# First block of a convolution and SiLU kernel: 64 by 64 convolution tiles, taps spread by transpositions, silu ahead of the weight splits

## The chip, the cores and the metric

The kernel runs on one core of a Trainium2 chip. The metric is the device time of one execution in microseconds; lower is better. The inputs are random with a fixed seed.

## The reference

`x` has 8 sequences of 4096 tokens with 192 channels. A causal depthwise convolution with 7 taps comes first, where 24 channels share one head's taps, normalized by a softmax; then an up projection to 2048, SiLU, and a down projection back to 192. The two projection weights come as float64.

```
w = softmax(weight, axis=-1)                     # (8 heads, 7 taps)
x_pad = concatenate([zeros(B, 6, D), x], axis=1)
x_unf = x_pad[:, idx, :].reshape(B, S, 7, 8, 24)  # 7 shifted views
conv = einsum('hk,bskhg->bshg', w, x_unf)         # (8, 4096, 192)
h = conv.reshape(32768, 192) @ w_in               # (32768, 2048)
out = (h * sigmoid(h)) @ w_out                    # (32768, 192)
```

## The kernel before

**Blocks.** The 32768 tokens are worked in blocks of 1024 (`TT`), each in two halves of 512 (`TB`). Channels lie on the partitions: the first 128 channels of a block in `nats[0]`, and the last 64, the tail, in `nats[1]`, with the two halves of the tokens on partitions 0 to 63 and 64 to 127. Tokens come from memory in 32 by 32 squares that VectorE transposes (`turn_in`). From block 1 on, a planned order written out as a string (`PLAN`) sets the order of every instruction; the up matmuls there use weights that were split into three parts (`w_a`, `w_b`), and fewer products by a fast matrix scheme. Block 0 is another path, ahead of the plan, and the change touches that path alone, but for the order of the channels in `load` and in the up weights.

**Block 0 now.** Its steps in program order, which each engine's queue keeps for its own share:

- The tap logits and the first 128 channels of 1024 tokens are loaded, the latter by four DMAs (two on SyncE's queue, two on ScalarE's), so that each of four partition groups `q` holds 256 tokens. Then SyncE loads the raw up weights for `j` = 0 to 3 (`load_in`; part 0 is the first 128 rows, part 1 the last 64) with the four tail loads between.
- Three heat matmuls on zeros (`heat`) run on TensorE. The softmax of the taps runs on VectorE and ScalarE; three small matmuls with selection matrices spread the taps over the channels (into `banks[6]` and `banks[7]`).
- `turn_q` transposes the four squares of channels into `x_q`; `diagonals` makes diagonal matrices of the taps; `conv_on_pe` runs the convolution of the first 128 channels on TensorE as 7 x 4 x 4 matmuls of 32 by 32, 256 columns each; `conv_taken` copies the four banks to `x_first[0]` on ScalarE. Every such float32 matmul appears as two records in the profile.
- The tail's convolution (`conv(0, 1, i)`) has its first tap on ScalarE and the other six on VectorE.
- The raw weights are float64 words that are rounded to float32 by integer operations: a `Unit` each for part 0 and part 1 of each `j` (units 0 to 7, even for part 0) and one for each quarter of the down weights (units 8 to 11). `work(u)` yields twice: first `begin(u + 1)` (exponent on VectorE and GpSimd, sign on ScalarE), mantissa and sticky of `u`, then `rounded` (three VectorE operations, the last writes `wd`), `top` on ScalarE and, for odd units, `spread`, two DMAs from one half of the partitions to the other. `split` makes the three parts for later blocks (two VectorE operations, one of ScalarE).
- `up_both(0)` runs the up matmuls of `j` = 0: eight banks with the first 128 channels, then the same banks with the tail, then eight silu on ScalarE. `up_first(j, c)` does four banks at a time for `j` = 1 to 3. All eight banks of PSUM are in use by `up_both`.
- The list `rest` (weight units 2 to 9 and their splits) and the list `ups` are merged by `woven`, by costs, into one program order. As written, `top` of units 2 and 3 and the first split come ahead of the silu of `up_both`.
- `down_plain` does the down matmuls of block 0, after which the plan begins with block 1.

```
ups = pieces(up_both(0), 72, 18, 18)
ups += [f for j in range(1, NJ) for c in (0, 2) for f in pieces(up_first(j, c), 36 - 9 * c, 18 + 9 * c)]
woven(rest, ups)
```

Nearly every instruction is issued through a helper, so the profile shows line 142 for all engines but TensorE, line 494 (`mm`) for matmuls and line 400 for `heat`; the tiles tell them apart (`nat`: x in rows, `xt`: x transposed, `wd`: rounded weights, `ps`: PSUM, `g`: silu results and scratch).

Of the kernel before, what the change touches and what calls it, by code (L numbers as in the profile page):

```python
# [8 lines left out]
F32 = mybir.dt.float32  # L9
# [9 lines left out]
def kernel(  # L19
# [166 lines left out]
    nats = [const.tile([P, n, SQ], F32, name=f"nat{i}") for i, n in enumerate((TT // SQ, TB // SQ))]  # L186
    TQ = TT // 4
    GQ = P // SQ
    x_q = const.tile([P, GQ, pad + TQ], F32, name="xt0")
    xts = [flat(x_q)[:, 0 : pad + TT], const.tile([P, pad + TB], F32, name="xt1")]  # L190
# [9 lines left out]
    def load(b, i, queue, cols=slice(0, None)):  # L200
        i, small = i % 4, i // 4
        dst = nats[small][SQ * i : SQ * i + SQ]
        if small:
            c = P + SQ * (i % 2)
            queue.dma_start(out=dst, in_=x_v[2 * b + i // 2][:, :, c : c + SQ])
        else:
            queue.dma_start(out=dst[:, cols], in_=x_w[b][:, cols, SQ * i : SQ * i + SQ])

    NG = D // SQ
    HG = H * NG  # L210
    nat_q = flat(nats[0]).rearrange("p (k g c) -> p k g c", g=GQ, c=SQ)
    wexp = const.tile([HG, K], F32, name="wexp")
    sync.dma_start(out=wexp, in_=weight.unsqueeze(0).to_broadcast([NG, H, K]))
    for q in range(4):
        src = x.flatten_outer_dims()[q * TQ : q * TQ + TQ, 0:P].rearrange("(k t) c -> t k c", t=SQ)
        to = flat(nats[0])[SQ * q : SQ * q + SQ].rearrange("p (k c) -> p k c", c=P)
        (act if q % 2 else sync).dma_start(out=to, in_=src)
# [7 lines left out]

    sel = const.tile([HG, NG + 2, SQ], F32, name="sel")
    sel_q = const.tile([HG, 4, SQ], F32, name="selq")
    mask = const.tile([HG, GQ], F32, name="mask")
    one_hot = const.tile([P, SQ], F32, name="hot")
    pool.memset(sel, 1.0)  # L230
    pool.memset(mask, 1.0)
    vec.memset(one_hot, 0.0)
    for sign in (1, -1):
        pool.affine_select(
            out=sel[:, 0:NG],
            in_=sel[:, 0:NG],
            compare_op=ALU.is_ge,
            fill=0.0,
            base=0 if sign > 0 else grp - 1,
            pattern=[[sign * (SQ + H * grp), NG], [sign, SQ]],  # L240
            channel_multiplier=-sign * grp,
        )
    for sign in (1, -1):
        pool.affine_select(
            out=mask,
            in_=mask,
            compare_op=ALU.is_ge,
            fill=0.0,
            base=0 if sign > 0 else H - 1,
            pattern=[[-sign * H, GQ]],  # L250
            channel_multiplier=sign,
        )
    for q in range(4):
        pool.affine_select(
            out=one_hot,
            in_=one_hot,
            compare_op=ALU.not_equal,
            fill=1.0,
            base=-SQ * q,
            pattern=[[-1, SQ]],  # L260
            channel_multiplier=1,
        )
    pool.memset(x_q[0:SQ, :, 0:pad], 0.0)
# [4 lines left out]
    in_a = moe_w_in.bitcast(I32)[0:P].rearrange("p (a m c) -> p a m c", a=2, c=2 * P)  # L268
# [145 lines left out]
    taps_all = banks[6][:, 0 : GQ * K].rearrange("p (g i) -> p i g", i=K)  # L414
    w_norm = const.tile([HG, K], F32, name="wnorm")
    spread_logits = const.tile([HG, GQ, K], F32, name="wspread")
    wred = const.tile([HG, 3], F32, name="wred")
    top, total, part_ = (wred[:, i : i + 1] for i in range(3))
    heat(3)
    vec.tensor_reduce(top, wexp, axis=AX.X, op=ALU.max, negate=True)  # L420
    act.activation(wexp, wexp, AF.Exp, bias=top, accum_out=total)
    act.activation(warm, warm, AF.Silu)
    vec.tensor_reduce(sel_q[:, 0, :], sel[:, 0:GQ, :].rearrange("r g c -> r c g"), axis=AX.X, op=ALU.add)
    vec.tensor_copy(sel_q[:, 1:4, :], sel_q[:, 0, :].unsqueeze(1).to_broadcast([HG, 3, SQ]))
    vec.tensor_copy(sel[:, NG : NG + 2, :], sel[:, NG - 2 : NG, :])
    vec.tensor_scalar(total, total, scalar1=1e-9, scalar2=None, op0=ALU.add)
    vec.reciprocal(part_, total)
    vec.scalar_tensor_tensor(
        out=spread_logits,
        in0=wexp.unsqueeze(1).to_broadcast([HG, GQ, K]),  # L430
        scalar=part_,
        in1=mask.unsqueeze(2).to_broadcast([HG, GQ, K]),
        op0=ALU.mult,
        op1=ALU.mult,
    )
    vec.tensor_scalar(w_norm, wexp, scalar1=part_, scalar2=None, op0=ALU.mult)
    pin(nc.tensor.matmul(banks[6][:, 0 : GQ * K], flat(sel_q), flat(spread_logits), start=True, stop=True))
    for k in (1, 0):
        of = flat(sel[:, 4 * k : 4 * k + 4, :])
        pin(nc.tensor.matmul(banks[7][:, K * k : K * k + K], of, w_norm, start=True, stop=True))  # L440
    heat(1)

    def turn_q(g):
        for g_ in (g, g + 1):
            vec.transpose(x_q[:, g_, pad:], nat_q[:, :, g_, :])
# [4 lines left out]
    turn_q(0)  # L450
    turn_q(2)
# [423 lines left out]
```

## Time and profile before

| | |
|---|---|
| median of 3 runs | 2237.4 us (2235.35 to 2238.51) |
| the profiled execution | 2236.91 us |
| its span, first to last instruction | 2235.2 us |
| mean granted TensorE clock | 0.999 |
| TensorE busy | 2218.2 us (99%) |
| VectorE busy | 1826.7 us (82%) |
| ScalarE busy | 1292.0 us (58%) |
| GpSimd busy | 50.6 us (2%) |

In the profile PE is TensorE's matmuls and PEld its weight loads, DVE is VectorE, ACT ScalarE, POOL GpSimd and SP SyncE, which here only issues DMAs; a q after the name stands for the engine's queue. Times count from the first instruction. A row of the timeline gives start, length, engine, line, operation, tiles (out<-in), shape, count, and in brackets the idle time before and what ended it; "issue" means nothing that the profile shows. Ends of matmuls are modelled, so rows overlap a little.

### The profile page before, as it was taken

How to read it: one execution, taken by the hardware profiler on the slowest of the kernel's cores; microseconds unless marked ns; L12 is line 12 of the kernel's file. 1: busy time of each engine (PE TensorE's matmuls, PEld its weight loads, DVE VectorE, ACT ScalarE, POOL GpSimd, SP SyncE). 2: the span in 40 equal slices, each digit the busy share in tenths (PEclk: the TensorE clock that was granted, in tenths of full speed). 3: DMA queues.
4: the chain of work that ended last, by engine and by line, in shares of the span. 5: the costliest groups of instructions: out<-in, count | busy, mean ns of one | idle time of the engine just before them, and what ended most of it. 6: DMA issues, size and time to landing. Idle time of an engine off the chain costs nothing.

```text
span 2235.2 us, 47341 instructions
## 1 busy us (share of the span) xinstructions
PE 2218.2 (99%) x19406; PEld 1632.6 (73%) x19406; DVE 1826.7 (82%) x3029; ACT 1292.0 (58%) x2648; POOL 50.6 (2%) x73
## 2 busy tenths in 40 slices
PE   8999999999999999999999999999999999999998
PEld 4377777777777777777777777777777777777776
DVE  8787888877888778888778887788887788877877
ACT  5267555666555675556665556755466654567543
POOL 4300000000000000000000000000000000000000
PEclk9999999999999999999999999999999999999999
DMA  4311011110011110111101111101111011111001
GB/s 130 69 25 29 6 26 29 30 30 15 16 30 29 30 29 6 26 29 30 30 14 17 30 29 30 29 3 28 30 29 30 13 18 29 29 29 30 3 14 29
DMA packets 405007, 61.77 MB, mean 28 GB/s; under 512 B 398134, under 2 KB 403254, under 8 KB 404790
## 3 DMA queue, kind: packets, MB, share of 16 engines
q1 hardware_dynamic: 401046, 58.10, 14.9%
q8 instruction: 151, 2.47, 0.5%
q10 hardware_dynamic: 3744, 0.66, 0.2%
q14 instruction: 66, 0.54, 0.1%
HBM read 31.46 MB, written 25.17 MB: 25 GB/s over the span
## 4 chain that ended last, share of the span: by engine, by line
PE 98%; DVE 1%; ACT 0%; issue 0%; ACTq 0%
PE ps L494 98%; DVE g L142 0%; DVE nat L142 0%; DVE wd L142 0%; DVE fin L142 0%; ACT nat L142 0%; DVE dot L142 0%; DVE w_a L142 0%; ACT ps L142 0%; ACT fin L142 0%; ACT w_a L142 0%; ACT g L142 0%; ACT w_b L142 0%; ACT xt L142 0%; ACTq L142 0%
## 5 line engine op out<-in xcount | busy, mean ns | idle before, releaser
L494 PE MATMUL ps<-g,wd 128*64 128x256 f32 (+1 forms) x10112 | 1125.6, 384 | 0.0
L494 PEld LDWEIGHTS ps<-g,wd 128*64 128x64 f32 x10112 | 720.4, 137 | 395.6 <-issue 34.1
L142 DVE TENSOR_TENSOR g<-g 128x1024 f32<-128x1024 f32 x806 | 951.5, 1219 | 9.2 <-PE ps L494 5.6
L494 PE MATMUL ps<-xs,w_a 64*128 64x512 f32 x5952 | 848.7, 390 | 1.3 <-DVE dot L142 0.9
L142 ACT ACTIVATE ps<-ps 128x512 f32<-128x512 f32 (+1 forms) x1085 | 569.9, 585 | 298.4 <-PE ps L494 252.0
L494 PEld LDWEIGHTS ps<-xs,w_a 64*128 64x128 f32 x5952 | 592.6, 184 | 108.6 <-DVE dot L142 14.8
L142 ACT ACTIVATE g<-ps 128x512 f32<-128x512 f32 x1024 | 562.2, 619 | 57.2 <-PE ps L494 50.1
L494 PE MATMUL ps<-xs,w_b 64*128 64x512 f32 x2976 | 501.0, 391 | 0.0
L142 DVE COPY dot<-ps 128x1 f32<-128x1 f32 x992 | 156.1, 157 | 353.9 <-PE ps L494 344.7
L142 DVE SCALAR_TENSOR_TENSOR nat<-xt,taps,nat 128x512 f32<-128x512 f32 (+1 forms) x378 | 373.5, 1002 | 5.1 <-ACT nat L142 4.6
L494 PEld LDWEIGHTS ps<-xs,w_b 64*128 64x128 f32 x2976 | 302.3, 184 | 53.0 <-issue 11.5
L142 ACT COPY fin<-ps 128x256 f32<-128x256 f32 (+1 forms) x127 | 47.9, 377 | 410.7 <-PE ps L494 410.7
L142 DVE TENSOR_TENSOR fin<-fin,ps 128x256 f32<-128x256 f32 x248 | 96.2, 407 | 17.0 <-PE ps L494 17.0
L142 DVE STREAM_TRANSPOSE fin<-fin 128x256 f32<-128x256 f32 (+1 forms) x189 | 83.4, 442 | 7.5 <-ACT fin L142 6.0
L142 ACT ACTIVATE nat<-xt,taps 128x512 f32<-128x512 f32 (+1 forms) x63 | 58.7, 935 | 16.0 <-DVE xt L142 14.6
L142 DVE STREAM_TRANSPOSE xt<-nat 128x1024 f32<-128x1024 f32 (+2 forms) x67 | 62.0, 930 | 2.6 <-DMA nat<-in_x_dram 2.5
L142 DVE TENSOR_TENSOR xs<-nat,xs 128x1024 fp32r<-128x1024 f32 (+1 forms) x62 | 59.0, 952 | 0.0
L142 DVE SCALAR_TENSOR_TENSOR xs<-xs 128x1024 fp32r<-128x1024 f32 (+1 forms) x62 | 59.0, 951 | 0.1
L142 ACT ACTIVATE xs<-nat 128x1024 fp32r<-128x1024 f32 (+1 forms) x62 | 52.5, 847 | 10.9 <-DVE nat L142 10.9
L142 ACT ACTIVATE fin<-ps 128x256 f32<-128x256 f32 x93 | 35.9, 386 | 39.0 <-PE ps L494 37.6
L494 PE MATMUL ps<-nat,wd 128*128 128x512 f32 (+1 forms) x128 | 44.7, 613 | 6.1 <-ACT g L142 4.7
L142 ACT COPY xt<-xt 64x6 f32<-64x6 f32 (+2 forms) x63 | 12.4, 197 | 64.5 <-DVE xt L142 63.7
(63 smaller groups left out, 257.3 us busy)
## 6 DMA issues: line engine op xcount, KB each, us to landing
out_dram<-fin SPq DMA_DIRECT2D x242, 96.0 KB, 2.5
nat<-in_x_dram SPq DMA_DIRECT2D x126, 128.0 KB, 2.9
nat<-in_x_dram SPq DMA_DIRECT2D x128, 64.0 KB, 2.2
g<-in_moe_w_out_dram SPq DMA_DIRECT2D x4, 384.0 KB, 4.3
w_b<-w_b SPq DMA_DIRECT2D x8, 192.0 KB, 3.0
fin<-in_moe_w_out_dram SPq DMA_DIRECT2D x4, 384.0 KB, 3.8
g<-in_moe_w_in_dram SPq DMA_DIRECT2D x2, 512.0 KB, 6.0
fin<-in_moe_w_in_dram SPq DMA_DIRECT2D x2, 512.0 KB, 8.2
```

Source lines behind the costliest of these rows:

```text
L142: return lambda *args, **kw: pin(getattr(self.engine, name)(*args, **kw))
L494: return pin(nc.tensor.matmul(to, lhs, rhs, start=start, stop=True, skip_group_check=True))
```

## The change

Five things change, all in or ahead of block 0:

1. The first 128 channels of block 0 are loaded as 64-channel rows into another layout (`nat_m`, `x_m`): partition group `i` holds token half `h` and channel half `s`. Each group comes in two DMAs, early (8 or 9 squares of 32 tokens) and late (8). The late ones of groups 0 and 2 are issued by SyncE behind the first `load_in`, those of groups 1 and 3 by ScalarE behind the Exp.
2. With this layout the channels of the first 128 stand in blocks of 32 in the order 0, 2, 1, 3 (`ORDER`); `load` and `load_in` part 0 follow it, and the latter becomes four DMAs of 32 partitions each instead of one of 128.
3. The taps are spread without matmuls: VectorE copies the logits to four partition groups, normalizes, transposes 32 by 32, copies along the channels of a head, and transposes again; GpSimd copies the results to `taps`. There are seven heat matmuls instead of three plus one.
4. The convolution on TensorE is 64 by 64: per token half (early, late) 7 x 2 x 2 matmuls of 256 columns, with seven separate diagonal instructions; the late transpositions stand between the two halves. `conv_taken` is called for banks 0 and 2, then, after the first tap of the tail and unit 0's rounding, for banks 1 and 3.
5. `up_both` with its silu comes whole ahead of the rest, with only the first piece of unit 2's work inside; the splits come later (`SPLIT_AFTER`), most of them behind unit 7.

```diff
+    ORDER = (0, 2, 1, 3)
+    TL = SQ + TB
+    nat_m = const.tile([P, TL // SQ, 2, SQ], F32, name="nat0")
+    x_m = const.tile([P, 2, TL], F32, name="xt0")
...
+    w32 = const.tile([P, SQ], F32, name="w32")
+    logits = w32[:, 0:K]
+    vec.memset(w32, 0.0)
+    sync.dma_start(out=w32[0:H, 0:K], in_=weight)
+
+    def load_first(i, late, queue):
+        h, s = divmod(i, 2)
+        lo, hi = (8, 16) if late else (-h, 8)
+        src = x.flatten_outer_dims()[TB * h + SQ * lo : TB * h + SQ * hi, R * s : R * s + R]
+        to = nat_m[SQ * i : SQ * i + SQ, 1 + lo : 1 + hi].rearrange("t k g c -> t k (g c)")
+        queue.dma_start(out=to, in_=src.rearrange("(k t) c -> t k c", t=SQ))
+
+    for i in range(4):
+        load_first(i, False, act if i % 2 else sync)
...
-            queue.dma_start(out=to, in_=in_a[:, :, 2 * j : 2 * j + 2, :])
+            for i in range(4):
+                of = in_a[ORDER[i], :, :, 2 * j : 2 * j + 2, :]
+                queue.dma_start(out=to[SQ * i : SQ * i + SQ], in_=of)
...
     load_in(0, 0, sync)
+    for i in (0, 2):
+        load_first(i, True, sync)
     for i in range(4, 8):
         load(0, i, sync)
     load_in(0, 1, sync)
...
-    heat(3)
+    heat(7)
+    for q in range(1, 4):
+        vec.tensor_copy(w32[SQ * q : SQ * q + H, 0:K], w32[0:H, 0:K])
+    vec.tensor_reduce(top, logits, axis=AX.X, op=ALU.max, negate=True)
+    act.activation(logits, logits, AF.Exp, bias=top, accum_out=total)
+    for i in (1, 3):
+        load_first(i, True, act)
     act.activation(warm, warm, AF.Silu)
...
+    vec.tensor_scalar(logits, logits, scalar1=part_, scalar2=None, op0=ALU.mult)
+    vec.transpose(turned, w32)
+    vec.tensor_copy(
+        by_channel.rearrange("p (h c) -> p h c", c=grp), turned[:, 0:H].unsqueeze(2).to_broadcast([P, H, grp])
     )
+    vec.transpose(flat(taps_all), by_channel)
+
+    def turn_first(late):
+        at_ = slice(9, 17) if late else slice(0, 9)
+        for g in range(2):
+            vec.transpose(x_m[:, g, SQ * at_.start : SQ * at_.stop], nat_m[:, at_, g, :])
...
-    def conv_on_pe():
+    def conv_on_pe(late):
         for i in reversed(range(K)):
-            for g in range(GQ):
-                for q in range(4):
-                    at_ = slice(SQ * q, SQ * q + SQ)
-                    to = banks[q][SQ * g : SQ * g + SQ, 0:TQ]
-                    mm(to, diags[at_, i, g, :], x_q[at_, g, i : i + TQ], i == K - 1)
-        homes.extend([homes.pop(0) for q in range(4)])
+            at_ = SQ - pad + i + HT * late
+            for g in range(2):
+                for h in range(2):
+                    to = rows(banks[2 * h + late], g)[:, 0:HT]
+                    w = rows(diags[:, i, g].rearrange("p s c -> p (s c)"), h)
+                    mm(to, w, rows(x_m[:, g, at_ : at_ + HT], h), i == K - 1)
...
-    conv_on_pe()
+    conv_on_pe(0)
+    turn_first(True)
+    conv_on_pe(1)
     begin(0)
     first_ = [work(u) for u in range(2)]
     next(first_[0])
+    for q in (0, 2):
+        conv_taken(q)
+    turn_in(0, 1)
+    halo_in(0, 2)
+    for q in range(4):
+        at_ = slice(SQ * q, SQ * q + SQ)
+        pool.tensor_copy(taps[at_, 1, :], taps_all[at_, 4 + q % 2, 0:K])
+        pool.tensor_copy(taps[at_, 0, :], taps_all[at_, ORDER[q], 0:K])
+    conv(0, 1, 0)
     next(first_[0])
-    for k in range(2):
-        vec.tensor_copy(taps[:, k, :], banks[7][:, K * k : K * k + K])
-    for q in range(4):
+    for q in (1, 3):
         conv_taken(q)
     units[0].top()
-    turn_in(0, 1)
-    halo_in(0, 2)
-    conv(0, 1, 0)
+    conv(0, 1, 1)
+    conv(0, 1, 2)
     next(first_[1])
-    for i in range(1, 4):
+    for i in range(3, 5):
         conv(0, 1, i)
     next(first_[1], None)
-    for i in range(4, K):
+    for i in range(5, K):
         conv(0, 1, i)
...
+    SPLIT_AFTER = {3: (1,), 4: (0,), 5: (3,), 6: (2,), 7: (5, 4, 7, 6)}
     for u in range(2, 2 * NJ):
-        rest += pieces_of_work(u) + [(units[u - 2].split, 8 if u % 2 else 14)]
-    rest += [(unit.split, 11) for unit in units[2 * NJ - 2 : 2 * NJ]]
+        rest += pieces_of_work(u)
+        rest += [(units[v].split, 8 if v % 2 else 14) for v in SPLIT_AFTER.get(u, ())]
...
     ups = pieces(up_both(0), 72, 18, 18)
-    ups += [f for j in range(1, NJ) for c in (0, 2) for f in pieces(up_first(j, c), 36 - 9 * c, 18 + 9 * c)]
-    woven(rest, ups)
+    for f, cost in (ups[0], rest[0], *ups[1:]):
+        f()
+    ups = [f for j in range(1, NJ) for c in (0, 2) for f in pieces(up_first(j, c), 36 - 9 * c, 18 + 9 * c)]
+    woven(rest[1:], ups)
```

More of the change, by code (lines that the diff above doesn't have):

```diff
@@ L198, in g_slot, with load @@
         return g_all[:, j // 2, 2 * c + n, j % 2, :]
-    def load(b, i, queue, cols=slice(0, None)):
+    def load(b, i, queue):
         i, small = i % 4, i // 4
@@ L223 @@
     act.activation(warm, warm, AF.Exp)
[L226 to L231, printed above, removed]
-    vec.memset(one_hot, 0.0)
[L233 to L252, printed above, removed]
-    for q in range(4):
+    one_hot = const.tile([P, R], F32, name="hot")
+    vec.memset(one_hot, 0.0)
+    for h in range(2):
         pool.affine_select(
@@ L413 @@
     taps = const.tile([P, 2, K], F32, name="taps")
[L414 to L417, printed above, removed]
+    taps_all = const.tile([P, NG, SQ], F32, name="taps_all")
+    turned = const.tile([P, SQ], F32, name="turned")
+    by_channel = const.tile([P, D], F32, name="by_channel")
     top, total, part_ = (wred[:, i : i + 1] for i in range(3))
-    heat(3)
@@ L436 @@
[L436 to L445, printed above, removed]
+    vec.tensor_scalar(logits, logits, scalar1=part_, scalar2=None, op0=ALU.mult)
@@ L451 @@
-    turn_q(2)
+    turn_first(False)
     def halo_in(b, i):
@@ L752, in up_both @@
             yield
-    for q in range(1, 4):
-        act.copy(x_q[SQ * q : SQ * q + SQ, :, 0:pad], x_q[SQ * q - SQ : SQ * q, :, TQ : TQ + pad])
-    diagonals(slice(K - 2, K))
-    diagonals(slice(0, K - 2))
+    for i in reversed(range(K)):
+        diagonal(i)
     for j in (1, 2, 3):
```

64 lines of the change are left out of this document (23 added, 41 removed).

## The prediction

> **What bounds the kernel now.** I read the page first, for the busy shares, then the chain of waits for the first 140 us, then each engine's timeline of the first 75 us, because the change touches the first block alone.
>
> ```profile
> PE 2218.2 (99%) x19406; PEld 1632.6 (73%) x19406; DVE 1826.7 (82%) x3029; ACT 1292.0 (58%) x2648; POOL 50.6 (2%) x73
> ```
>
> TensorE is busy for nearly all of the 2235.2 us span, so a change in the first block is worth what it moves of the moment from which TensorE no longer waits. The chain of waits (start, length, what) tells that moment:
>
> ```profile
> 33.25 0.49 ACT g L142
> 33.75 0.04 issue
> 33.79 75.12 PE ps L494 x288
> ```
>
> From 33.79 on TensorE runs 75.12 us without a break; what was ahead of it was a silu of ScalarE. TensorE's timeline (start, length; in brackets the idle time before and who ended it):
>
> ```profile
> 1.12 2.93 PE L400 MATMUL ps<-zeros 128*128 128x256 f32 x6 [1.12 <-DVE hot L142]
> ...
> 7.67 6.60 PE L494 MATMUL ps<-xt,g 32*32 32x256 f32 x209
> 16.11 0.66 PE L494 MATMUL ps<-xt,g 32*32 32x256 f32 x15 [1.84 <-issue]
> 17.52 7.13 PE L494 MATMUL ps<-nat,wd 128*128 128x512 f32 x16 [0.74 <-ACT nat L142]
> 25.36 3.77 PE L494 MATMUL ps<-nat,wd 64*128 64x512 f32 x16 [0.70 <-DVE nat L142]
> 33.79 33.74 PE L494 MATMUL ps<-nat,wd 128*128 128x512 f32 x96 [4.66 <-ACT g L142]
> ```
>
> In order: heat matmuls, the convolution, the first part of `up_both` (17.52), its second part (25.36), then 4.66 us of nothing, then the six `up_first`. TensorE was done at 29.13, and all eight banks waited for their silu. ScalarE's timeline says why:
>
> ```profile
> 28.95 0.63 ACT L142 ACTIVATE w_a<-wd 128x512 fp32r<-128x512 f32 x1 [5.10 <-DVE wd L142]
> ...
> 32.84 0.42 ACT L142 ACTIVATE w_b<-wd 128x256 fp32r<-128x256 f32 x1 [1.84 <-DVE wd L142]
> 33.16 2.04 ACT L142 ACTIVATE g<-ps 128x512 f32<-128x512 f32 x4
> ```
>
> ScalarE takes its work in program order, and `top` of weight units 2 and 3, which wait for VectorE, stood ahead of the silu at 33.16. The gap costs a second time, in stretches of the span (length, busy time of PE, PEld, DVE, ACT, POOL, then granted clock, DMA share, GB/s):
>
> ```profile
> 7.60:12.70 5.10, 5.10 (x167) 3.82 (x168) 3.70 (x9) 1.14 (x2) 0.97 (x1) 1.00 0.64 164
> 12.70:14.30 1.60, 1.57 (x71) 0.92 (x43) 1.56 (x5) 0.00 (x0) 1.52 (x2) 1.00 1.04 279
> ...
> 33.20:36.60 3.40, 2.81 (x4) 1.25 (x5) 3.33 (x7) 3.40 (x9) 3.24 (x3) 0.50 0.15 39
> ```
>
> From 33.20 to 36.60 the granted clock is 0.50. TensorE works 2.81 us of that at half speed and loses 1.4 us.
>
> **The change, part by part.** VectorE carries the first 30 us, so I walk along its timeline.
>
> ```profile
> 5.26 1.42 DVE L142 STREAM_TRANSPOSE xt<-nat 128x256 f32<-128x256 f32 x4
> 6.61 1.12 DVE L142 TENSOR_TENSOR g<-hot,ps 128x256 f32<-128x256 f32 x2
> 8.80 1.69 DVE L142 TENSOR_SCALAR g<-g 128x512 int32<-128x512 int32 x4 [1.08 <-DMA g<-in_moe_w_in_dram]
> ...
> 11.34 0.29 DVE L142 TENSOR_SCALAR g<-g 128x256 int32<-128x256 int32 x1 [0.25 <-DMA g<-in_moe_w_in_dram]
> ...
> 13.10 0.69 DVE L142 SCALAR_TENSOR_TENSOR wd<-g 128x512 f32<-128x512 f32 x1
> 13.71 0.23 DVE L142 COPY taps<-ps 128x7 f32<-128x7 f32 x2
> ...
> 15.00 0.63 DVE L142 TENSOR_SCALAR g<-g 128x512 int32<-128x512 int32 x2 [0.45 <-DMA g<-in_moe_w_in_dram]
> ...
> 19.61 2.33 DVE L142 SCALAR_TENSOR_TENSOR nat<-xt,taps,nat 128x512 f32<-128x512 f32 x3 [3.20 <-ACT nat L142]
> ...
> 22.64 0.43 DVE L142 SCALAR_TENSOR_TENSOR wd<-g 128x256 f32<-128x256 f32 x1
> 22.98 2.32 DVE L142 SCALAR_TENSOR_TENSOR nat<-xt,taps,nat 128x512 f32<-128x512 f32 x3
> ...
> 28.22 0.69 DVE L142 SCALAR_TENSOR_TENSOR wd<-g 128x512 f32<-128x512 f32 x1
> ...
> 32.38 0.42 DVE L142 SCALAR_TENSOR_TENSOR wd<-g 128x256 f32<-128x256 f32 x1
> ```
>
> *Taps.* Three tap matmuls, the masks and five VectorE operations for them go. In their place come three copies of 8 by 7 (0.12 each, as the two taps copies, 0.23) and three operations of up to 192 columns (at most 0.36 each, a quarter of the 1.42). Counted from 5.26 the first transposition starts at 5.3 to 6.7; I take 6.3, near the upper end since all are in series. The early transpositions have 576 of 1024 columns: 0.8, to 7.1. Seven diagonals instead of two instructions, same columns: 1.12 plus five starts of about 0.1, so the first is there at 7.3 and the last at 8.7. The late transpositions (512 columns) take 0.7, to 9.4 if their data are there.
>
> *Loads.* SyncE's queue and the landings (KB each, then median us from issue to landing), the one long issue by itself first:
>
> ```profile
> 5.70 2.62 SPq L142 DMA_DIRECT2D g<-in_moe_w_in_dram  x1
> ```
>
> ```profile
> 5.70 5.20 SPq L142 DMA_DIRECT2D g<-in_moe_w_in_dram  x5
> 10.94 4.90 SPq L142 DMA_DIRECT2D fin<-in_moe_w_in_dram  x6
> 23.09 1.15 SPq L142 DMA_DIRECT2D wd<-wd  x2
> ```
>
> ```profile
> wd<-wd SPq DMA_DIRECT2D x8, 64.0 KB, 2.0
> nat<-in_x_dram ACTq DMA_DIRECT2D x2, 128.0 KB, 2.9
> ```
>
> Without its long one, the five at 5.70 take 0.65 each, whether of 512 or 128 KB. Cutting `load_in` part 0 in four adds 12 issues and the late rows 2 on SyncE. Ahead of the late rows stand four instead of one, so they are issued by about 6.2 and land 2.9 later, at 9.1; if each issue takes 0.82 (the six at 10.94), at 10.5. The two late loads on ScalarE's queue, behind the Exp, are at about the same place. So VectorE ends the late transpositions between 9.4 and 11.2; I take 10.2, and unit 0 begins there instead of at 8.80.
>
> The Trainium skill, page "DMA: Bandwidth & Descriptors", section "Rules for kernel authors", speaks against this part: transfers to separate halves of the partitions share the same 16 DMA engines, so one transfer over 128 partitions is better. By that rule the quarters bring no bandwidth and only issues, and the load part is a loss that case (a) below prices at 2232.1. The rows agree that an issue costs about the same for 512 KB as for 128.
>
> *VectorE from unit 0 to the convolution of the tail.* Before, it is 8.80 to 25.30, 16.5 us, of which idle 0.25, 0.45 and 3.20, and 0.2 for the taps copies, which go to GpSimd: 12.4 of work, 12.6 with joins. The 3.20 goes, because the tail's first tap on ScalarE no longer stands behind `conv_taken` of all four banks and `top`. So: unit 0's weights at 10.2 + 5.5 = 15.7 (before 13.79; one transposition moved ahead), the tail finished at 22.8 (25.30), unit 1's weights at 21.3 (23.07), since two taps now follow it instead of three. GpSimd's eight small copies are bounded by
>
> ```profile
> L142 POOL COPY xt<-xt 128x6 f32<-128x6 f32 x23 | 5.4, 233 | 1492.3 <-DVE dot L142 1363.1 <-ACT g L142 68.4 <-DVE nat L142 60.8
> ```
>
> 0.23 each, 1.9 in all from about 6.6: done well ahead of the 13 at which the first tap reads them.
>
> *Convolution on TensorE.* One 256-column record a tile took 16 of 167 in 5.10 us, 0.49 a round, until 12.7, and 0.27 or less after: the first is half the rate of the second although the granted clock shows 1.00 in both. (`up_both` gives 0.446 for 512 columns, 0.223 for 256.) With four tiles instead of sixteen a tile runs 28 rounds instead of 14: 6.2 at the fast rate, 12 to 14 at the slow one. The fast rate came 5.1 us after unbroken work began at 7.6; with seven heat matmuls (7 x 0.98 by the first row) unbroken work begins at 1.12 and the fast rate is due near 6.2, so the heats end by 7.0 and I take 6.2 for the convolution: early half 7.3 to 10.4, late half 10.4 to 13.5. Then `conv_taken`: inputs there by 15, under the weights' 15.7. The Trainium skill, page "TensorE: Matmul & The Clock Gate", section "Part 1: The HAM clock gate (the "warmup" mystery)", has the array at half clock until one window of about 3.4 us was busy, the windows running freely. By it (an estimate from that page) the fast rate is there at 7.9 at the latest, and rival (b) cannot happen; the trace shows the two rates but not seven heats, so (b) keeps a small chance.
>
> The 1.84 of "issue" lay after 223 records and has no counterpart here: the change has 112.
>
> *First part of `up_both`* therefore starts at 15.7 (17.52), ends at 22.9.
>
> *Second part* needs the tail (22.8) and the spread of unit 1, 2.0 after its issue. SyncE reaches that only after the 14 added issues: 15.84 + 14 x 0.6 = 24.2 with the stalls of now (5.20 + 4.90 less 11 x 0.63 is 3.2 of them), 21 without. So 23.3 to 26.2; I take 24.0 (before 25.36).
>
> *Silu first.* Second part to its end 3.6: 27.6. Unit 2's weights come 3.6 after the tail, 26.4; banks come free from about 26. `up_first` starts at 27.6 instead of 33.79: **6.2 us**. No split lies between units 2 and 3 any more, whose two operations of 512 columns (0.69 each) are in the 32.80 - 28.91 = 3.9 of now; so unit 3 is there at 26.4 + 2.5 = 28.9, its spread at 30.9, wanted at 31.2: no wait, though it is the next thing late (I allow 0.2). Without a gap over 4 us the clock does not drop: **1.4 us**.
>
> *Splits later.* Their work is the same; they move behind units 2 to 7. Nobody but block 1 reads them.
>
> *Does it reach the end?*
>
> ```profile
> 67.47 41.42 PE L494 MATMUL ps<-g,wd 128*64 128x512 f32 x192
> ```
>
> ```profile
> 59.20 1.40 DVE L142 SCALAR_TENSOR_TENSOR wd<-g 128x768 f32<-128x768 f32 x1
> ...
> 107.86 2.40 DVE L142 STREAM_TRANSPOSE fin<-fin 128x512 f32<-128x512 f32 x3 [6.00 <-ACT fin L142]
> ```
>
> The down matmuls would start at 60; unit 8's weights, 60.60 before, come 2.5 earlier with VectorE, 58.1. At 107.86 VectorE had idled 6.00; with its own 2.5 it covers 8.5. Both covers hold; were VectorE not earlier at all, 6.0 would be the cap.
>
> Sum: 6.2 + 1.4 - 0.2 = **7.4 us**. The profiled execution took 2236.91 (1.7 around its span), so 2229.5; the median of the three runs is 0.5 above it, so **2230.0**.
>
> **The rivals.** (a) *The prologue gives nothing*, the added issues eating what the missing 3.20 wait gave: second part at 25.4, `up_first` at 29.0, a wait of 0.9 for unit 3's spread: 4.8 + 1.4 - 0.9 = 5.3, 2232.1. For it: 14 more issues on a queue that stalled twice. (b) *The convolution stays at the slow rate*: 7.3 + 12, copies 0.6, first part at 19.9, second at 27.0, `up_first` at 30.6: 3.2 + 1.4 = 4.6, 2232.8. Against it: the heats. (c) *The gap only changes its owner*: the silu is early but another producer (late weights of unit 2 or 3) holds TensorE as long; only the clock's 1.4 stays, 2236.0. Against it: unit 2 is ready at 28.91 even now. (d) *Slower: the load queue backs up.* Five added issues stand ahead of unit 1's load, on which VectorE waits before it can round unit 0. At 2.62 each, the long one, instead of 0.6 they delay it by 10.1; it would land near 12 and is wanted near 13.4, so it is 8.7 late, and the nine further ones press on units 2 to 5 with about 2 more: 2237.4 - 7.4 + 10.7 = 2240.7. It decides from 2.4 us an issue (5 x 1.8 = 1.4 + 7.4). For it: that issue was taken behind 128-byte tails, which still stand in the queue; against: only two of 11 stalled.
>
> **How the numbers follow.** 0.2% is 4.5 us, about what a measurement of this kernel can tell from no change. Chances: forecast 0.62, (a) 0.17, (b) 0.05, (c) 0.06, (d) 0.10. Faster by over 4.5: nearly all of the first, most of (a), half of (b): 0.75. Same: the rest of these and (c): 0.13. Slower: (d) and an unnamed remainder: 0.12. Of the unknown costs, a second part at 26.2 gives 5.2; late transpositions ending at 9.4 bring VectorE 0.8 earlier and the spread to 22.5, which gives 8.9, 2228.5. The range goes from 2228.4 to 2236.0: it holds (a), (b) and (c) and leaves (d) and the remainder out.
>
> **What would show it.** Right: no `up_first` gap over 1 us, silu at about 25.5, a granted clock of 1.00 between 27 and 40, down matmuls starting at 60. Each step: unit 0 beginning on VectorE near 10.2, the convolution ended near 13.5 at 0.22 a round, second part near 24. Wrong: a wait of VectorE for the late rows beyond 12, long issues on SyncE, or a new TensorE wait at the start of block 1 near 101.

## The result and the profile after

The changed kernel takes 2231.31 us (median of 17 runs, 2230.17 to 2233.13), the kernel before on the same chip 2236.5 (median of 17). The ratio is 0.9981, 95% interval [0.9973, 0.9988]: faster by 5.2 us. The forecast was 7.4 less, 2230.0 with a range from 2228.4 to 2236.0. The profiled execution of the changed kernel took 2232.93 (span 2231.1) beside 2236.91 before, so what follows accounts for 4.0 of time, or 4.1 of span; why that is less than the medians show comes with the third fence. In two of the later runs (`signs_again`, `all_three`) one execution was slow, at 2825 and 4622 us; it is left out of their medians.

TensorE's timeline of the changed kernel (start, length, operation and count; in brackets the idle time ahead and who ended it):

```profile
6.58 6.46 PE L478 MATMUL ps<-xt,g 64*64 64x256 f32 x112 [0.47 <-DVE g L142]
15.30 8.22 PE L478 MATMUL ps<-nat,wd 128*128 128x512 f32 x18 [2.26 <-DMA g<-in_moe_w_in_dram]
25.26 37.57 PE L478 MATMUL ps<-nat,wd 64*128 64x512 f32 x110 [1.74 <-issue]
62.76 41.42 PE L478 MATMUL ps<-g,wd 128*64 128x512 f32 x192
106.84 1.20 PE L478 MATMUL ps<-xs,w_a 64*128 64x512 f32 x8 [1.53 <-DVE dot L142]
```

The wait of 4.66 for a silu is gone: from 25.26 the second part of `up_both` and the six `up_first` run in one piece. The down matmuls start at 62.76 instead of 67.47, 4.7 earlier. Two waits are new or longer. Two matmuls of the second part (the last two of the 18 in the second row, which end at 23.52) ran, and then TensorE stood until 25.26. And at the start of block 1 it waits 1.53 for `dot` of VectorE; before, the same wait was 0.68, at 110.70. So 4.7 less 0.85 is 3.9 of the 4.1.

ScalarE's timeline shows that the silu is early, and what now stands behind it:

```profile
23.56 0.60 ACT L142 ACTIVATE g<-ps 128x512 f32<-128x512 f32 x1 [1.88 <-PE ps L478]
27.34 1.08 ACT L142 ACTIVATE g<-ps 128x512 f32<-128x512 f32 x2 [3.18 <-PE ps L478]
28.86 2.56 ACT L142 ACTIVATE g<-ps 128x512 f32<-128x512 f32 x5 [0.43 <-PE ps L478]
...
31.79 0.69 ACT L142 ACTIVATE g<-fin 128x512 int32<-128x512 uint8 x1
```

The eight silu start at 23.56 and end at 31.4; before, they began at 33.16. The last row is the `sign` of weight unit 4, an operation that VectorE needs: it now comes after all eight.

The half-clock stretch didn't go, it moved into the second part (length, busy time of PE, PEld, DVE, ACT, POOL, granted clock, DMA share, GB/s):

```profile
21.68:25.09 3.41, 1.85 (x4) 0.29 (x2) 3.38 (x6) 0.60 (x2) 2.37 (x2) 1.00 0.78 197
25.00:29.00 4.00, 3.74 (x10) 1.84 (x12) 3.86 (x9) 1.22 (x3) 2.79 (x3) 0.57 0.57 190
```

The clock was 0.50 from 25.09 to 28.50. This differs from execution to execution: two further profiles of the same kernel, `after_again` and `after_third` below, have no such stretch and took 2231.26 and 2231.77. Of the 17 times above, 13 lie from 2230.17 to 2231.81 and four from 2232.93 to 2233.13; the profiled execution is one of the four.

VectorE's timeline:

```profile
5.56 0.79 DVE L142 STREAM_TRANSPOSE xt<-nat 128x288 f32<-128x288 f32 x2
6.28 1.47 DVE L142 TENSOR_TENSOR g<-hot,taps_all 128x128 f32<-128x128 f32 x7
8.97 0.77 DVE L142 STREAM_TRANSPOSE xt<-nat 128x256 f32<-128x256 f32 x2 [1.23 <-DMA nat<-in_x_dram]
9.67 1.64 DVE L142 TENSOR_SCALAR g<-g 128x512 int32<-128x512 int32 x4
...
14.40 0.69 DVE L142 SCALAR_TENSOR_TENSOR wd<-g 128x512 f32<-128x512 f32 x1
...
20.47 0.42 DVE L142 SCALAR_TENSOR_TENSOR wd<-g 128x256 f32<-128x256 f32 x1
20.82 1.53 DVE L142 SCALAR_TENSOR_TENSOR nat<-xt,taps,nat 128x512 f32<-128x512 f32 x2
...
32.51 0.69 DVE L142 SCALAR_TENSOR_TENSOR fin<-fin,g 128x512 int32<-128x512 int32 x1 [1.72 <-ACT g L142]
...
38.12 0.45 DVE L142 SCALAR_TENSOR_TENSOR fin<-fin,g 128x256 int32<-128x256 int32 x1 [0.99 <-ACT g L142]
...
43.45 0.69 DVE L142 SCALAR_TENSOR_TENSOR fin<-fin,g 128x512 int32<-128x512 int32 x1 [1.80 <-ACT g L142]
...
60.32 1.40 DVE L142 SCALAR_TENSOR_TENSOR wd<-g 128x768 f32<-128x768 f32 x1
...
78.97 1.83 DVE L142 STREAM_TRANSPOSE xt<-nat 128x1024 f32<-128x1024 f32 x2
...
104.52 1.90 DVE L142 STREAM_TRANSPOSE fin<-fin 128x512 f32<-128x512 f32 x3 [0.87 <-ACT fin L142]
```

Up to 22 us VectorE is ahead of the kernel before (tail finished at 22.35 instead of 25.30). Then it waits three times for a `sign` behind the silu, 4.5 in all. Block 1's first transpositions begin at 78.97; before:

```profile
77.87 1.83 DVE L142 STREAM_TRANSPOSE xt<-nat 128x1024 f32<-128x1024 f32 x2
```

The lead of about 3 us is lost, and VectorE enters block 1 later than before by 1.1. That it is later goes with the half-clock stretch, which pushes the silu back and the signs with them: in the two profiles without it VectorE waits 2.4 and 2.6 for signs and enters block 1 at 77.16 and 77.25, 0.7 and 0.6 earlier than before. Its idle time ahead of the `fin` transpositions has shrunk from 6.00 to 0.87. That is as low as it gets, as the chain into it shows:

```profile
102.93 0.71 DVE L142 STREAM_TRANSPOSE xt<-nat 128x512 f32<-128x512 f32 x1 [0.61 <-DMA nat<-in_x_dram]
```

```profile
103.68 0.20 ACT L142 COPY xt<-xt 64x6 f32<-64x6 f32 x1 [8.06 <-DVE xt L142]
103.90 1.56 ACT L142 COPY fin<-ps 128x512 f32<-128x512 f32 x3
```

VectorE's last transposition for block 2 waits for its load; ScalarE's small halo copy waits for the transposition; ScalarE's copies of block 0's output stand behind the halo copy; and VectorE's `fin` transpositions need the first of these. So the start of block 1 hangs on when VectorE gets there and on when that load lands.

Last, the queue of SyncE and the time to landing of the spreads between 20 and 30 us:

```profile
14.62 7.62 SPq L142 DMA_DIRECT2D fin<-in_moe_w_in_dram  x12
22.36 1.16 SPq L142 DMA_DIRECT2D wd<-wd  x2
```

```profile
DMA to landing us min/median/max: 2.0/2.4/2.8
```

Unit 1's weights are there at 20.89 (VectorE's row at 20.47), but SyncE issues loads, 0.64 each, until 22.24. The spread goes out at 22.36 and its first half lands at 25.17, 2.8 later; TensorE goes on at 25.26.

### The profile page after: what moved, and what is told of

Read it like the earlier page. It is cut to its first block, busy times and chain, and to the rows that moved or that the text cites. A ratio compares the mean times of both kernels' runs of the same rounds, so it can differ in the third digit from the quotient of the medians.

```text
span 2231.1 us, 47153 instructions
## 1 busy us (share of the span) xinstructions
PE 2217.9 (99%) x19294; PEld 1642.9 (74%) x19294; DVE 1825.8 (82%) x3035; ACT 1287.9 (58%) x2643; POOL 50.3 (2%) x73
## 2 busy tenths in 40 slices
DMA packets 406313, 61.79 MB, mean 28 GB/s; under 512 B 400464, under 2 KB 404560, under 8 KB 406096
## 3 DMA queue, kind: packets, MB, share of 16 engines
HBM read 31.47 MB, written 25.17 MB: 25 GB/s over the span
## 4 chain that ended last, share of the span: by engine, by line
PE 95%; DVE 1%; SPq 0%; issue 0%; DMA 0%; ACT 0%; DVEq 0%
PE ps L478 95%; DVE nat L142 1%; DVE g L142 0%; SPq L142 0%; DVE wd L142 0%; DVE fin L142 0%; DVE xt L142 0%; DMA nat<-in_x_dram 0%; DMA out_dram<-fin 0%; ACT nat L142 0%; DVE xs L142 0%; DVE dot L142 0%; ACT fin L142 0%; ACT ps L142 0%; ACT xt L142 0%
## 5 line engine op out<-in xcount | busy, mean ns | idle before, releaser
L478 PEld LDWEIGHTS ps<-xs,w_a 64*128 64x128 f32 x5952 | 601.9, 184 | 102.1 <-DVE dot L142 15.5
L478 PE MATMUL ps<-xs,w_b 64*128 64x512 f32 x2976 | 506.5, 392 | 0.0
L478 PEld LDWEIGHTS ps<-xs,w_b 64*128 64x128 f32 x2976 | 308.7, 184 | 49.2 <-issue 11.5
L142 DVE STREAM_TRANSPOSE xt<-nat 128x1024 f32<-128x1024 f32 (+3 forms) x67 | 62.0, 928 | 4.5 <-DMA nat<-in_x_dram 4.5
L142 ACT COPY xt<-xt 64x6 f32<-64x6 f32 x58 | 11.3, 195 | 66.3 <-DVE xt L142 65.7
```

The lines of the kernel that those rows point to most:

```text
L142: return lambda *args, **kw: pin(getattr(self.engine, name)(*args, **kw))
L478: return pin(nc.tensor.matmul(to, lhs, rhs, start=start, stop=True, skip_group_check=True))
```

## The experiments

Two theories. The **TensorE theory**: the time that TensorE regains in the first 60 us arrives whole at the end, and what is missing from the forecast is the stop at 25.26 and the clock. The **seam theory**: the silu ahead of the signs makes VectorE late, and its chain into block 1 takes back part of what TensorE gained. Differences are between medians, with the kernel before run on the same chip (2237.75 in the first four runs, 2237.6 in the next four, 2236.64 in the last three).

### The order alone

`silu_only`: the kernel before with the two parts of `up_both` ahead of the weave and the splits later; the prologue is the old one.

```
+    SPLIT_AFTER = {3: (1,), 4: (0,), 5: (3,), 6: (2,), 7: (5, 4, 7, 6)}
...
+    for f, cost in (ups[0], rest[0], *ups[1:]):
+        f()
...
-    woven(rest, ups)
+    woven(rest[1:], ups)
```

> The kernel before with only the order changed (silu of up_both ahead of the rest, splits later). Both theories: first and second part of up_both stay at 17.5 and 25.4, up_first begins near 29.0 instead of 33.79, with about 0.9 of wait for unit 3's spread. TensorE theory (what TensorE regains arrives at the end): 3.5 to 5.3 us faster than before. Seam theory (VectorE's work for block 1 caps the gain, because ScalarE's silu now stand ahead of the signs that VectorE waits for): VectorE has no early start here, so its work ends at 78 to 80 instead of 77.9, which leaves a cap of 4 to 6: 3.5 to 4.5 us.

Measured: 2232.92, 0.9982 [0.9972, 0.9991], 4.8 less than before. TensorE:

```profile
24.91 36.96 PE L494 MATMUL ps<-nat,wd 64*128 64x512 f32 x112 [0.69 <-DVE nat L142]
61.79 41.42 PE L494 MATMUL ps<-g,wd 128*64 128x512 f32 x192
...
105.88 1.19 PE L494 MATMUL ps<-xs,w_a 64*128 64x512 f32 x8 [1.54 <-DVE dot L142]
```

The order by itself closes the gap and brings the down matmuls 5.7 earlier, to 61.79, about as early as the whole change does. The wait of 1.54 at block 1 comes with it, so it needs no new prologue. Nor does it need a wait for a sign: VectorE has none here and enters block 1 at 78.28, 0.4 later than before, while TensorE comes 5.7 earlier.

### The prologue alone

`front_only`: the changed kernel with the old order (the edit above, backwards).

> The changed kernel with the old order of silu and splits. Both theories: unit 0 and the tail as in the changed kernel (9.7 and 22.4), second part of up_both waiting for unit 1's spread until about 25.2, up_first waiting for the silu behind top of unit 3 until about 31 instead of 33.79. 2.8 us faster than before if the clock drops once as before, 4.2 if it doesn't. The seam caps nothing, since VectorE is 2.9 early and never waits for a sign.

Measured: 2231.98, 0.9979 [0.9970, 0.9989], 5.8 less than before. TensorE:

```profile
15.09 8.22 PE L478 MATMUL ps<-nat,wd 128*128 128x512 f32 x18 [1.46 <-ACT nat L142]
...
30.61 34.06 PE L478 MATMUL ps<-nat,wd 128*128 128x512 f32 x96 [1.68 <-ACT g L142]
64.60 41.42 PE L478 MATMUL ps<-g,wd 128*64 128x512 f32 x192
...
107.83 1.19 PE L478 MATMUL ps<-xs,w_a 64*128 64x512 f32 x8 [0.67 <-DVE dot L142]
```

VectorE is earlier, so the same `top` waits end earlier and the silu gap is 1.68 instead of 4.66; the down matmuls come 2.9 earlier, and the seam takes nothing (0.67): VectorE waits for no sign and enters block 1 at 74.69, 3.2 earlier than before. The median is better than the 2.8 to 4.2 expected. This profile, which has a half-clock stretch at 31.18, took 2233.23, 3.7 less than before, and not 5.8. By either measure the halves do not add up (2.9 and 5.7 at the down matmuls, where the whole change has 4.7, or 6.4 without its stretch; 5.8 and 4.8 in the medians, where it has 5.2): both shorten the same gap. Once it is closed by the order, an earlier first part of `up_both` (15.30 instead of 17.08 in `silu_only`) ends at the stop at 25.26.

### The stop filled with work

`filled_gap`: five matmuls of zeros in `up_both`, behind the first matmul of the second part, so that TensorE isn't idle ahead of 25.

```
+                    if c == n == 0:
+                        for _ in range(5):
+                            mm(to[0, 0][:, 0 : 2 * P], zeros, zeros.unsqueeze(1).to_broadcast([P, 2, P]))
```

> The changed kernel with five matmuls of zeros added to a bank of up_both (they add zero) behind the first matmul of its second part, so that TensorE isn't idle from 22.9 to 25.2. Granted clock 1.00 from 20 to 40 instead of 0.5 from 25.1 to 28.5; down matmuls starting at 61.2 instead of 62.8. TensorE theory: 1.6 us faster than the changed kernel, 6.8 faster than before. Seam theory: at most 0.4 faster than the changed kernel, 5.2 to 5.6 faster than before, with a longer TensorE wait at the start of block 1.

Measured: 2232.10, 0.9978 [0.9969, 0.9987], 5.6 less than before.

```profile
23.49 2.42 PE L478 MATMUL ps<-zeros 128*128 128x256 f32 x10
25.84 35.99 PE L478 MATMUL ps<-nat,wd 64*128 64x512 f32 x110
```

The theories expected 6.8 and 5.2 to 5.6 less than before. No half-clock stretch, but the zeros delay the second part by 0.6, to 25.84. The run doesn't tell the theories apart: the changed kernel also has executions without a stretch, as the next one.

### The changed kernel again

`after_again` and `after_third`, unchanged, in the second and the third set of runs.

> The changed kernel once more, to have it on the same chip as the next three. 4 to 5 us faster than before. The second part of up_both held until about 25.2 by unit 1's spread, TensorE's wait at the start of block 1 about 1.5; where the clock drops by half for 3.4 us depends on the execution.

> The changed kernel once more, to stand beside the two others on the same chip. Both theories: 4 to 5.5 us less than the kernel before.

Measured: 2232.49, 0.9982 [0.9973, 0.9992], and 2231.33, 0.9978 [0.9969, 0.9987]: 5.1 and 5.3 less than before. TensorE of `after_third`, and the stretch ahead of its second part; then TensorE at block 1 and VectorE's last transposition for block 2 in `after_again`:

```profile
25.17 35.96 PE L478 MATMUL ps<-nat,wd 64*128 64x512 f32 x110 [1.72 <-issue]
61.06 41.42 PE L478 MATMUL ps<-g,wd 128*64 128x512 f32 x192
...
105.17 1.19 PE L478 MATMUL ps<-xs,w_a 64*128 64x512 f32 x8 [1.56 <-DVE dot L142]
```

```profile
21.60:25.10 3.50, 1.85 (x4) 0.29 (x2) 3.46 (x6) 0.61 (x2) 2.45 (x2) 1.00 0.66 168
```

```profile
104.38 1.19 PE L478 MATMUL ps<-xs,w_a 64*128 64x512 f32 x8 [0.86 <-DVE dot L142]
```

```profile
100.47 0.71 DVE L142 STREAM_TRANSPOSE xt<-nat 128x512 f32<-128x512 f32 x1 [0.34 <-DMA nat<-in_x_dram]
```

The stop is there again, the half-clock stretch is not: the same 110 matmuls take 35.96 instead of 37.57, so the stretch costs 1.6. The down matmuls start 6.4 earlier than before; less the 0.88 more at block 1, that makes 5.5, where the profiled times differ by 5.1.

The wait at block 1 is not the same in each execution of one kernel. In `after_again` the down matmuls start at 60.98 and VectorE enters block 1 at 77.16, each within 0.1 of `after_third`, but the wait is 0.86 instead of 1.56. The difference of 0.7 is in the loads of block 2: VectorE waits 2.23 and 0.34 for the last two in `after_again`, 2.37 and 0.89 in `after_third`. Block 1 here starts 6.3 earlier than before.

### The signs ahead

`signs_ahead`: `sign` of unit 4 between the two halves of the silu, and a written-out order in which the second piece of the first `up_first` calls (`10b`, `12b` and so on, each with four silu) stands a turn later, behind the sign that the next unit's work begins with. `signs_again` is the same kernel; what its expectation calls the bottoms of the splits are these second pieces.

```
-    for f, cost in (ups[0], rest[0], *ups[1:]):
+    for f, cost in (ups[0], rest[0], ups[1]):
         f()
+    units[4].sign()
+    signed.add(4)
+    ups[2][0]()
...
-    woven(rest[1:], ups)
+    SEQUENCE = (
+        "2b 10a 3a 3b s1 4a 10b 12a 4b s0 5a 12b 5b 20a s3 6a 20b 6b s2 22a 7a 7b 22b s5 s4 s7 s6 "
+        "30a 8a 8b 30b 32a 9a 32b 9b"
+    )
+    for name in SEQUENCE.split():
+        called[name]()
```

> The changed kernel with sign of unit 4 between the two halves of up_both's silu, and the silu of up_first behind the next unit's sign. VectorE's waits for a sign (1.72, 0.99 and 1.80 at 32.5, 38.1 and 43.5) gone or under 0.5 each. Seam theory: VectorE is 4 us earlier at 79, the wait of TensorE at the start of block 1 goes from 1.53 back to 0.7, 0.9 us faster than the changed kernel, 6.1 than before. TensorE theory: same as the changed kernel, 5.2 than before.

> The kernel with the sign of unit 4 between the two halves of the silu and the bottoms of the splits one turn later, once more. TensorE theory (with VectorE's waits for the signs gone, the whole of the earlier start reaches the end): 2 to 3 us less than the changed kernel in the same call, 7 to 8 less than the kernel before; down matmuls near 61. Seam theory: 0.9 less than the changed kernel, and the 7.5 of the first run was scatter of the steady state.

Measured: 2230.23, 0.9970 [0.9959, 0.9980], 7.5 less than before; and again 2230.85, 0.9977 [0.9968, 0.9987], 5.8 less than before and 0.5 less than `after_third` beside it. ScalarE in `signs_ahead`, and TensorE in `signs_again`:

```profile
27.67 0.69 ACT L142 ACTIVATE g<-fin 128x512 int32<-128x512 uint8 x1
```

```profile
25.52 35.96 PE L478 MATMUL ps<-nat,wd 64*128 64x512 f32 x110 [0.42 <-issue]
61.41 41.42 PE L478 MATMUL ps<-g,wd 128*64 128x512 f32 x192
...
104.64 1.19 PE L478 MATMUL ps<-xs,w_a 64*128 64x512 f32 x8 [0.69 <-DVE dot L142]
```

The sign of unit 4 comes at 27.67 instead of 31.79, VectorE's three waits for signs are gone, and the wait at block 1 is 0.89 and 0.69. But VectorE was expected 4 us earlier at block 1, and it is not: the one wait for `w_b`, another operation of ScalarE, grew from 0.61 to 1.78 and 2.09, and VectorE enters block 1 at 76.68 and 77.12. That is 15.7 behind the start of the down matmuls, where all three profiles of the changed kernel have 16.2. So the silu ahead of the signs are a part of the cause of the longer wait, worth about 0.5, as between the medians of `signs_again` and `after_third`. That they are all of it is not shown: with the signs behind, `after_again` waits 0.86, and `silu_only`, where VectorE waits for no sign, 1.54.

That the first run seemed to bring 2.4 more than the changed kernel was not confirmed: there the two stood beside the kernel before in different sets of runs. From the start of block 1 to the last matmul the 13 profiles of this document take from 2118.1 to 2120.1, with TensorE idle for 0.6 in each; so the pace of the later blocks scatters by 2 us without a wait, and `signs_ahead`, with 2118.2, got 1.2 of its lead over `after_again`, with 2119.4, from there. In `signs_again` a half-clock stretch at 15.3, in the first part, took back part of the 0.87 that the seam gained on `after_third`.

### The spread ahead of a load

`j3_later`: the load for `j` = 3 (weight units 6 and 7; six of the twelve issues at 14.62) is issued behind the spread of unit 1 instead of with the early ones.

```
-    for j in (1, 2, 3):
+    for j in (1, 2):
...
+    for part in (0, 1):
+        load_in(3, part, sync)
```

> The changed kernel with the six loads of the raw weights of j = 3 issued behind the spread of unit 1 instead of ahead of it. Both theories of the start: SyncE is free at 18.4, so the spread is issued as soon as unit 1 is rounded (20.9) and lands at 22.9; second part of up_both without a break near 22.9, up_first at 26.5 at full clock. TensorE theory: all of it arrives, 3.5 to 4 us faster than the changed kernel. Seam theory: the silu come 2 to 3 us earlier too, so VectorE waits less for the signs (1.72 and 1.80 under 0.7) and is about 3 us earlier at 76, so 2.5 to 3.5 faster than the changed kernel, part being lost in a TensorE wait at block 1 that stays over 1.2.

Measured: 2231.58, 0.9977 [0.9967, 0.9986], 6.0 less than before and 0.9 less than `after_again` beside it, short of the 2.5 to 4 expected. The timeline and two stretches:

```profile
15.25 44.73 PE L478 MATMUL ps<-nat,wd 128*128 128x512 f32 x128 [2.00 <-ACT nat L142]
59.91 41.42 PE L478 MATMUL ps<-g,wd 128*64 128x512 f32 x192
```

```profile
11.97:15.38 3.41, 1.41 (x23) 0.90 (x16) 3.38 (x7) 2.07 (x6) 2.21 (x2) 1.00 0.55 155
15.38:18.79 3.41, 3.41 (x5) 1.35 (x6) 3.34 (x7) 0.89 (x2) 2.35 (x2) 0.50 0.68 209
```

From 15.25 on TensorE stops nowhere. By itself that doesn't show that the stop was SyncE's queue, because this execution had its half-clock stretch in the first part, which ends later for it: `seam_later`, with its loads unchanged and a stretch from 16.25 to 19.66, shows no stop either. But its up matmuls take 45.72, 1.0 more than the 44.73 here, which is what the queue still costs there. `both`, below, shows it without a stretch. The down matmuls start at 59.91, at the 60 of the forecast. The times of `j3_later` and `after_again` overlap (2230.68 to 2232.16, and 2231.14 to 2234.26).

### VectorE's turn to block 2 later

`seam_later`: the transposition for block 2 that stood ahead of block 0's output is put behind it.

```
-    for t in (*loads_, *turns):
+    for t in (*loads_, *turns[:2]):
...
+    for t in turns[2:]:
+        step(2, t)
```

> The changed kernel with the last transposition of block 2's tail and the two small halo copies around it (ScalarE) placed behind the copies and transpositions of block 0's output instead of ahead of them. Seam theory: ScalarE copies the output as soon as TensorE has it (102.6 instead of 103.90), TensorE's wait at the start of block 1 goes from 1.53 to 0.7, 0.8 to 0.9 us faster than the changed kernel. TensorE theory: the same as the changed kernel within 0.3.

Measured: 2232.66, 0.9983 [0.9973, 0.9992], 4.9 less than before, no better than `after_again`. VectorE:

```profile
103.56 0.67 DVE L142 STREAM_TRANSPOSE xt<-nat 128x512 f32<-128x512 f32 x1
...
104.45 0.15 DVE L142 COPY dot<-ps 128x1 f32<-128x1 f32 x1
```

The moved transposition (0.67 at 103.56) now stands between `fin` and `dot`, and TensorE waits 1.28 for `dot`. So this form of the seam theory fell: moving work at the seam itself gives nothing, since the same work stays ahead of `dot`. VectorE has to arrive earlier, as in `front_only` (0.67) and with the signs ahead.

### Both mended

`all_three`: signs ahead, the load for `j` = 3 behind the spread (the expectation of `both` calls it unit 3's, and speaks of two further edits where the heat is the only one), and four more heat matmuls ahead of `up_both`. `both`: the same without the heat.

> Three edits on the changed kernel: the loads of j = 3 behind the spread, the signs ahead of the silu, and four heat matmuls between the convolution and up_both, so that TensorE has no idle time over 0.7 us from 6.6 to 60. Granted clock 1.00 from 7 on. Second part near 22.9, up_first 26.5, down matmuls at 58.8 if unit 8's weights are there (VectorE's work ends 4 to 5 us earlier than in the changed kernel, at 74). Seam theory: 4 us faster than the changed kernel, with the wait at block 1 near 0.7 to 0.9; TensorE theory: 4 as well. It tells whether the two sources are all there is.

> The signs ahead and the load of unit 3 behind the spread of unit 1, without the two further edits of the run all_three. TensorE theory: second part of up_both near 22.7 to 24.0 without a stop, up_first near 27, down matmuls near 59.5, and 1 us less than with the signs ahead alone. Seam theory: the same start, but a TensorE wait of 0.7 to 1.5 at the start of block 1 and the same time as with the signs ahead alone within 0.5.

Measured: 2231.22, 0.9974 [0.9965, 0.9984], 6.4 less than before and 1.3 less than `after_again` beside it, where 4 were expected; and 2230.01, 0.9972 [0.9962, 0.9983], 6.6 less than before and 1.3 less than `after_third` beside it. TensorE and SyncE of `both`:

```profile
15.15 44.98 PE L478 MATMUL ps<-nat,wd 128*128 128x512 f32 x128 [2.00 <-ACT nat L142]
60.06 41.42 PE L478 MATMUL ps<-g,wd 128*64 128x512 f32 x192
...
103.30 1.19 PE L478 MATMUL ps<-xs,w_a 64*128 64x512 f32 x8 [0.68 <-DVE dot L142]
```

```profile
20.77 1.15 SPq L142 DMA_DIRECT2D wd<-wd  x2
```

The spread goes out at 20.77 instead of 22.36, TensorE doesn't stop, the wait at block 1 is that of the kernel before, and this execution had no half-clock stretch. It beats both kernels: all seven of its times (2229.72 to 2230.59) lie under the lowest of `after_third` (2230.87). It is 0.8 better than the signs ahead alone in the same set, near the 1 of the TensorE theory, and, level with `all_three`, the best of the versions that ran beside the changed kernel. Its block 1 starts at 103.30, 7.4 earlier than before.

So each theory has its share. The stop at 25 us costs 0.9 net (`j3_later`), the signs 0.5 net (`signs_again`), together 1.3 (`both`); only the last of these has no time in common with the changed kernel beside it. In the traces the stop is worth about 1 us of TensorE's start, and the seam takes from 0.2 to 0.9, of which the signs explain about 0.5 and the landing of a load up to 0.7; the half-clock stretch, which comes and goes, blurs both in the times. What is regained up to the start of block 1 is kept: TensorE's idle time behind it is 0.6 before and in every version.

## Why the prediction was right, and where its steps were off

The main mechanism was right: the gap of 4.66 went, because the silu no longer stood behind `top` of units 2 and 3 (`silu_only` and `front_only` part the two), and 5.2 of the forecast 7.4 arrived. What the runs gave lies nearest to the price of rival (a), 5.3 less, which had a chance of 0.17, and its account of the second part is the one that came true. In `after_third` the sum reads: second part at 25.17 and 3.6 long, so `up_first` 5.0 earlier instead of 6.2; 1.4 for the clock; less 0.9 at block 1 instead of 0.2: 5.5. In the profiled execution the new stretch takes 1.6 more, and 3.9 is left.

- *Taps, diagonals, GpSimd's copies.* First transposition 5.56 (forecast 6.3), diagonals from 6.28 (7.3), GpSimd's copies 1.50 long (1.9). Sized slightly too high. (The idle 1.84 of the convolution before, which this part puts behind 223 records, stands behind 209 in the row; nothing hangs on it.)
- *Late rows.* VectorE waited 1.23 for them and began unit 0 at 9.67 (10.2, bounds 9.4 to 11.2). Right.
- *VectorE to the tail.* Unit 0's weights at 15.1 (15.7), unit 1's at 20.89 (21.3), tail finished at 22.35 (22.8). Right.
- *Convolution on TensorE.* 6.46 (6.2), from 6.58 to 13.04. Right; rival (b), 12 or more, is out.
- *First part of `up_both`.* 15.30 (15.7), but it ends at 22.4 only to stop.
- *Second part.* This is the term of the sum that was mis-sized: it runs from 25.26, 25.17 and 25.09 in three profiles, within the bounds of 23.3 to 26.2 but 1.1 to 1.3 behind the 24.0 taken. The issue was nearly as forecast (22.36, where 24.0 less 2.0 is 22.0); but unit 1's weights, ready at 20.89, had then waited 1.5 for the queue, and the landing took 2.8 instead of 2.0. That is what rival (a) says, added issues eating what VectorE gained, and `both` shows it by taking six of the issues away. (a)'s further 0.9, a wait for unit 3's spread, didn't come.
- *Silu first.* ScalarE's silu came at once behind TensorE, as forecast. But the step priced the move by TensorE and the banks alone. The splits were not all that the silu were moved past: the signs of the later units stand in the same queue, and the step did not name them. VectorE then waited 1.72, 0.99 and 1.80 for signs, and 0.61 for `w_b`; under the old order, in `front_only`, it waited for neither.
- *No clock drop.* Wrong in the first profile, right in the two others. The 1.4 was sized well (1.6 measured), but its premise, a drop only behind a gap over 4 us, failed: a gap of 1.74 was enough in one execution, and gaps of 1.72 and 1.60 had no drop in two others. Whether each execution of the kernel before pays the 1.4 isn't shown.
- *Does it reach the end.* Here a step failed. "Unit 8's weights come 2.5 earlier, 58.1" was 61.72, only 1.0 ahead of the down matmuls; VectorE came to block 1 at 78.97, 1.1 later than before, instead of 2.5 earlier, and 0.6 to 0.7 earlier in the two other profiles. The cap of 6.0 for a VectorE that isn't earlier didn't hold either: with 4.7 gained 0.85 was already given back. The idle time of 6.00 ahead of `fin` was not all cover: 0.87 of it is the halo copy and the first output copy, which follow VectorE's transposition whatever TensorE does (0.87 or 0.88 in all profiles but those of the kernel before, `front_only` and `seam_later`), so that about 5.1 was cover; and the landing of a load moves the end of the chain by up to 0.7. A wait of about 0.7 remains even where VectorE is early (0.68 before, 0.67 in `front_only`, 0.68 in `both`).
- *Rivals (c) and (d).* (c) is out: no producer held TensorE as long. (d) is out: the load issues stayed at 0.64 to 0.73, far from the 2.4 from which it decides.

## What to carry to other kernels

When work is moved ahead on an engine that takes its queue in order, list what it is moved past and who waits for each of these, up to the next seam; here eight silu delayed three signs, and most of a lead of 3 us was gone by block 1. Idle time of an engine is cover only less what must follow its last operation in the chain. A small transfer with a deadline shouldn't stand behind a burst of loads on the same issuing queue, even where the loads are not urgent. Two edits that close the same gap are worth about one of them, and a gain near the scatter must be measured beside its rival in the same set of runs.

## What the runs showed of the hardware

The clock can drop behind a stretch in which TensorE was partly busy. In the kernel before, TensorE was idle for the whole 3.41 us ahead of the drop at 33.20. In the later profiles with a drop, the 3.41 us ahead of it had TensorE busy for 1.85 (the changed kernel, 21.68 to 25.09) and 1.41 (`j3_later`, 11.97 to 15.38), and each time the clock was 0.50 for just 3.41. A like share, 1.85 of 3.50, had no drop in `after_third`, and a smaller one, 1.60 of the 3.41 from 11.44 to 14.85, had none in the changed kernel's own profile. So the share alone doesn't decide it, and whether the same gap costs 1.6 is open until the run; that it hangs on where the gap falls in a free-running window is argued, not tested. The Trainium skill, page "TensorE: Matmul & The Clock Gate", section "Part 1: The HAM clock gate (the "warmup" mystery)", has the clock fall back after at least one idle window of about 3.4 us, and windows that run freely; the length agrees with these rows, the idleness does not, since TensorE was 54% and 41% busy in the windows ahead of the drops.

The first half of the spread, a transfer of 64 KB inside the core, took 2.8, 3.2 and 3.1 us to land in the three profiles of the changed kernel, where twelve loads are issued just ahead of it, and 1.9 in `j3_later` and `both`, where six of them are issued behind it (there the second half, with these loads right behind, took 3.4). The issue of a load held SyncE 0.64 us (7.62 for 12), so that twelve of them hold the queue for longer than the first part of `up_both` runs (7.13 before).
